# A fused causal convolution and multiplicative FFN on one core: order of the prologue's loads and first parts, and the place of the third convolution slot

## The chip, the core and the metric

One of the eight NeuronCores of a Trainium2 chip runs the whole program. Its engines run side by side and meet only at semaphores: the matrix engine (PE, with its weight loads shown apart as PEld), the vector engine (DVE), the scalar engine (ACT), GpSimd (POOL) and the sync engine (SP), which here only issues transfers. PE writes its results into PSUM; DVE and ACT carry them from there into SBUF, the working memory. The metric is the time of one execution on the device, in microseconds (us).

## The reference

```python
w = softmax(weight, over the 7 taps)                  # 8 heads x 7 taps
x_pad = zeros of 6 rows ahead of x                    # x: 8 x 3904 x 192
conv[b,s,h,:] = sum_k w[h,k] * x_pad[b,s+k,h,:]       # 24 channels a head
a = conv @ w1                                         # 192 -> 1024
b = conv @ w2                                         # 192 -> 1024
out = ((a * b) @ w3) @ w_out                          # 1024 -> 1024 -> 192
```

There are 31232 rows (tokens) of 192 channels. Inputs and output are float32; the kernel computes in bf16 with float32 sums. It multiplies w3 by w_out once (`W_sb`, 1024x192), so that a row needs two products: the first (`a` and `b`, and their elementwise product `abT`) and the second (`abT` by `W_sb`).

## The kernel before

**Tiles.** The rows are cut into two streams of 15616 (`NS = 2`), which lie on partitions 0 to 63 and 64 to 127. A *round* `R` is 512 rows of each stream; there are 31 rounds, in groups of four. The convolution works on *windows* of 64 rows, of which 58 are new, held in *blocks* of 6, 4, 8, 10, 8, six times 36, and 20 windows. It is a matmul too: per head a banded 64x64 matrix (`Aband`) times the window's 24 channels.

**The order is written by hand** (`tc.manual_schedule()`, line 65): each engine runs its instructions, and each queue its transfers, in the order of the program.

**PSUM** is one tile, `pairs`, of four pairs of banks. `banks()` (line 71) takes the first free pair off a list, `drained()` (line 78) appends it at the end when the code that empties it has been written.

**The prologue** (lines 136 to 560). The small `weight` is loaded (line 137), turned into a softmax by DVE and ACT (lines 216 to 224) and spread by a matmul; `diag`, a diagonal made by two selects on POOL (line 176), is multiplied by the taps (`band`, line 245) and summed by matmuls into `Aband`. The first quarter of w1 and w2 comes as float32 (`wfirst`, line 164) and is cast by ACT and POOL (`cast_w`); the other quarters come through POOL's queue (`load_w`), which also loads x (`load_x0`, line 171; `load_x`, line 105), all these with a cast. Block 0 is convolved (line 515) and transposed by PE into `xT` (line 517). Then, from line 521:

```python
    move_all(*conv(1, 0, H, "streams"), (A, V))
    first_tile(0)
    first_part(0, [0], 0, EARLY)
    move_all(*joint_transposes(1), (A, A, V))
    first_part(0, [1], 0, EARLY)
    first_part(0, [0, 1], EARLY, CH)
```

Block 1 is convolved and transposed here; `first_part` (line 403) is one part of a first product for columns of w1 and w2 in blocks of 128: two factors on PE (`first_factor`, twelve matmuls in all), a cast of the first by ACT (`first_cast`, line 386) and the product of the two by DVE (`first_times`, line 393). `EARLY` is 348, the rows of block 0. Blocks 2 to 4 are convolved among the first products of rounds 0 to 2. w3 is cast by a transfer into `w3rows`, and SP transposes it back in 16 pieces (`w3_transposes`, line 459). At line 557 POOL copies two values of `w3T`, which makes POOL wait for that piece before it issues the loads of blocks 5 and 6. `w3_product` (line 464) makes `W_sb`.

**The main loop** (line 579). A group has four first products (32 parts), then eight second products, one for each round and stream. Block `6 + p` is convolved in group `p`, head by head (`conv_heads`, line 566), in three *slots* of three, three and two heads, each placed behind one of the eight second products by `at` (line 590); DVE empties each head's pair. Behind the last slot the block is stored to `rows` in DRAM by SP (`store`); SP transposes it from there into `xT` during the next group (`send`, `transposes`), for the group after. Block 5 is convolved in the first group as well, behind its first three second products.

Of the kernel before, what the change touches and what calls it, by code (L numbers as in the profile page):

```python
# [16 lines left out]
def kernel(  # L17
# [10 lines left out]
    nc = tc.nc  # L28
# [49 lines left out]
    def drained(p):  # L78
        assert p not in free
        free.append(p)  # L80
# [53 lines left out]
                tiles.append((xb, 0))  # L134

    wall = const.tile([1, H, K], FP32)
    nc.scalar.dma_start(out=wall, in_=weight.rearrange("(o h) k -> o h k", o=1))

    n0 = SIZES[0] // 2
    xb0 = work.tile([128, 2 * n0, D], BF16, tag="xb", bufs=5, name="xb")  # L140
# [8 lines left out]
    diag = const.tile([128, Q + PAD], BF16)  # L149
    nc.vector.memset(zeros, 0.0)  # L150
    nc.vector.memset(tiny, 0.0)
    nc.vector.memset(ones, 1.0)  # L152
    nc.vector.memset(xb0[:, 0, :], 0.0)
    nc.vector.memset(half, 0.0)
    nc.vector.memset(half[:, Q:2 * Q], 1.0)
# [4 lines left out]
    wd = [const.tile([128, NP, DFF], BF16, name=f"wd{i}", tag=f"wd{i}") for i in range(2)]  # L160
    w_rows = [w.rearrange("(k q) f -> q k f", q=Q) for w in (moe_w1, moe_w2)]

    for i in range(2):
        nc.sync.dma_start(out=wfirst[:, i], in_=w_rows[i][:, :, 0:WC[1]])

    def load_w(part):
        cs = slice(WC[part], WC[part + 1])
# [3 lines left out]
    def load_x0(r):  # L171
        nc.gpsimd.dma_start(out=xb0[Q * r:Q * r + Q, 1:, :], in_=x_spans(r, 1, 2 * n0 - 1))  # L172

    load_x0(0)
    for p0 in (0, Q):
        nc.gpsimd.affine_select(  # L176
            out=diag[p0:p0 + Q], in_=ones[p0:p0 + Q].to_broadcast([Q, Q + PAD]),
            pattern=[[-1, Q + PAD]], compare_op=ALU.is_equal, fill=0.0, base=0,
            channel_multiplier=1)
    load_x0(1)  # L180
    for r in range(NS):
        nc.gpsimd.dma_start(out=xb0[Q * r + PAD:Q * r + Q, 0, :],  # L182
# [20 lines left out]
    def warm(n):  # L203
# [5 lines left out]

    warm(6)  # L210

    wmax = const.tile([1, H], FP32)
    wsum = const.tile([1, H], FP32)
    wrow = const.tile([1, H, K], BF16)
    wsb = const.tile([128, 2, 2, K], BF16)
    nc.vector.reduce_max(out=wmax, in_=wall, axis=AX.X)
    nc.vector.tensor_tensor(
        out=wall, in0=wall, in1=wmax.unsqueeze(2).to_broadcast([1, H, K]), op=ALU.subtract)
    nc.scalar.activation(out=wall, in_=wall, func=ACT.Exp)
    nc.vector.tensor_copy(out=ident[0:Q, 0:Q], in_=diag[0:Q, 0:Q])  # L220
    nc.vector.reduce_sum(out=wsum, in_=wall, axis=AX.X)
    nc.vector.reciprocal(out=wsum, in_=wsum)
# [268 lines left out]
    def move_all(p, moves, fs):  # L491
        for f, m in zip(fs, moves):
            move(f, m)
        drained(p)
# [22 lines left out]
    for k, f in enumerate((V, V, A)):  # L517
        p, *m = pe_transpose(0, k)
        move(f, m)
        drained(p)  # L520
    move_all(*conv(1, 0, H, "streams"), (A, V))
    first_tile(0)
    first_part(0, [0], 0, EARLY)
    move_all(*joint_transposes(1), (A, A, V))
    first_part(0, [1], 0, EARLY)
    first_part(0, [0, 1], EARLY, CH)
    load_w3(0)
    for i in range(2):
# [25 lines left out]
        3: seq([(pe_transposes, 4)])})  # L554
    store(4, need(GROUP - 1) - 1, queue=nc.gpsimd)
    nc.gpsimd.dma_start(out=wo_b, in_=wor)
    P(out=pace, in_=w3T[0:1, JT // 2 - 1, DFF - 2:DFF])
    load_x(5)
    load_x(6)
    first_product(3)  # L560
# [18 lines left out]
    for p, rounds in enumerate(groups):  # L579
        b = PROLOGUE_BLOCKS + p  # L580
        order = rounds[-1:] + rounds[:-1] if rounds[-1] == NR - 1 else rounds
        for j, R in enumerate(order if p else ()):
            first_product(R)
            send(R + GROUP)
            if j < 2 and b < NB:
                P(out=pace, in_=abT_of[R][0:1, JT - 1, 1, 0:2])  # L586
                load_x(b, (j,))
        if b < NB:
            zero(b)
        at = {1: [(b, slots[0])], 3: [(b, slots[1])], 5: [(b, slots[2])]}  # L590
        if p == 0:
            at = {0: [(5, slots[0], (V, A))], 1: [(5, slots[1], (V, A))],
                  2: [(5, slots[2], (V, A), need(GROUP))], 4: at[1], 5: at[3], 6: at[5]}
        for i, (R, r) in enumerate((R, r) for R in rounds for r in range(NS)):
            second_product(R, r, R == NR - 1 and r == 1, nc.sync if p else nc.gpsimd)
            for c in at.get(i, ()) if b < NB else ():
                conv_heads(*c)
            if p == 0 and i == 2:
                send(2 * GROUP - 1)
# [31 lines left out]
```

## Time and profile before

| | |
|---|---|
| runs shown | 521.29, 521.9, 522.05 us; median 521.9 |
| profiled execution | 522.07 us, of which the span from the first to the last instruction is 520.4 |
| granted PE clock | 1.00 |
| busy share of the span | PE 99%, PEld 65%, DVE 69%, ACT 63%, POOL 11% |
| DMA | 64.61 MB, mean 124 GB/s |

In the rows of the timeline stand the start in us, the time over which a merged row runs, the engine, the line and the operation, what is written and read, how many instructions the row merges, and in brackets the idle time ahead of it with what ended that. "POOLq", "SPq" and "ACTq" rows are instructions that a queue issues and that don't count as busy. In the chain of waits each piece has its start, its length and its name. Neighbouring matmuls overlap, so their distances are read from start to start.

### The profile page before, as it was taken

The numbers are of one execution on the slowest core, as the hardware profiler recorded it, in microseconds if no ns is written. First come the engines' busy times: TensorE is split into PE (matmuls) and PEld (weight loads), VectorE is DVE, ScalarE is ACT, GpSimd is POOL, SyncE is SP. The second block draws the span as 40 slices with busy tenths as digits, with TensorE's granted clock in tenths as the row PEclk, the third lists the DMA queues.
The fourth block names the chain that finished last, engine by engine and source line by source line (L and its number), as shares of the span: only waits on it lengthen the run. The fifth ranks groups of instructions, "written<-read, shape, count | busy, mean of one in ns | idle before, by whom it ended". The sixth has DMA issues, their size and how long they took to land.

```text
span 520.4 us, 13006 instructions
## 1 busy us (share of the span) xinstructions
PE 513.5 (99%) x5576; PEld 339.8 (65%) x5576; DVE 357.5 (69%) x343; ACT 325.7 (63%) x410; POOL 58.4 (11%) x98
## 2 busy tenths in 40 slices
PE   8999999999999999999999999999999999999997
PEld 4455788455885558845588455884558855599567
DVE  6778646899538994389943899438993299911970
ACT  6887643777437774377743777337774377734762
POOL 8501522130000200002000010001200000000000
PEclk9999999999999999999999999999999999999999
DMA  9979998699656973569645699456724532024004
GB/s 116 169 142 126 163 222 208 162 186 166 143 146 161 116 94 113 146 161 128 82 116 147 155 122 89 118 146 157 103 44 122 155 96 32 17 94 151 1 3 152
DMA packets 133420, 64.61 MB, mean 124 GB/s; under 512 B 90304, under 2 KB 132642, under 8 KB 133298
## 3 DMA queue, kind: packets, MB, share of 16 engines
q1 hardware_dynamic: 94320, 44.06, 36.1%
q0 software_dynamic: 38896, 19.62, 30.4%
q8 instruction: 43, 0.70, 0.6%
q14 instruction: 15, 0.12, 0.1%
q10 hardware_dynamic: 146, 0.10, 0.1%
HBM read 33.25 MB, written 36.52 MB: 134 GB/s over the span
## 4 chain that ended last, share of the span: by engine, by line
PE 95%; ACT 1%; DVE 1%; DMA 1%; POOL 1%; issue 0%; POOLq 0%; ACTq 0%
PE pairs L381 59%; PE pairs L432 32%; PE pairs L290 3%; DVE abT L400 1%; PE pairs L467 1%; ACT asb L389 1%; DMA xb<-in_x_dram 1%; PE pairs L343 0%; POOL xb L172 0%; POOL xb L182 0%; ACT convo L311 0%; POOL xb L119 0%; ACT xT L355 0%; POOL diag L176 0%; PE pairs L507 0%
## 5 line engine op out<-in xcount | busy, mean ns | idle before, releaser
L400 DVE TENSOR_TENSOR abT<-asb,pairs 128x1024 bf16<-128x1024 bf16 (+1 forms) x245 | 298.1, 1217 | 76.8 <-ACT asb L389 60.5
L381 PE MATMUL pairs<-xT,wd 64*128 64x512 bf16 (+3 forms) x3000 | 319.7, 371 | 0.7 <-DVE abT L400 0.3
L389 ACT CAST asb<-pairs 128x1024 bf16<-128x1024 f32 (+1 forms) x245 | 247.1, 1009 | 67.7 <-PE pairs L381 67.3
L381 PEld LDWEIGHTS <-wd 64*128 64x128 bf16 x3000 | 162.3, 94 | 151.8 <-issue 1.8
L432 PE MATMUL pairs<-W_sb,abT 128*128 128x192 bf16 x1952 | 166.1, 246 | 0.0
L432 PEld LDWEIGHTS <-abT 128*128 128x128 bf16 x1952 | 159.6, 98 | 9.7 <-issue 9.7
L437 ACT COPY osb<-pairs 128x384 f32<-128x384 f32 x122 | 58.3, 478 | 116.0 <-PE pairs L432 116.0
L311 DVE CAST convo<-pairs 128x864 bf16<-128x864 f32 (+5 forms) x67 | 50.8, 815 | 67.6 <-PE pairs L290 67.6
L119 POOL DMA_DIRECT2D xb<-in_x_dram x42 | 32.2, 781 | 7.6 <-PE pairs L381 4.1
L586 POOL COPY pace<-abT 1x2 bf16<-1x2 bf16 x10 | 1.7, 174 | 238.7 <-DVE abT L400 238.7
L290 PE MATMUL pairs<-xb,Aband 64*64 64x432 bf16 (+5 forms) x384 | 17.5, 284 | 0.4 <-DMA xb<-in_x_dram 0.3
L290 PEld LDWEIGHTS <-Aband 64*64 64x64 bf16 x384 | 7.2, 106 | 7.5 <-issue 6.3
L311 ACT CAST convo<-pairs 128x512 bf16<-128x512 f32 (+4 forms) x15 | 8.1, 584 | 0.5 <-PE pairs L290 0.4
L444 POOL DMA_DIRECT2D out_dram<-osb x8 | 6.1, 758 | 18.4 <-ACT osb L437 18.4
L437 DVE COPY osb<-pairs 128x192 f32<-128x192 f32 x1 | 0.4, 358 | 11.1 <-PE pairs L432 11.1
L467 PEld LDWEIGHTS <-w3T 128*128 128x128 bf16 x64 | 5.2, 98 | 0.4 <-issue 0.4
L467 PE MATMUL pairs<-wo_b,w3T 128*128 128x192 bf16 x64 | 5.5, 246 | 0.0
L190 POOL COPY wd<-wd 64x768 bf16<-64x768 bf16 x6 | 4.8, 847 | 0.0
L206 PE MATMUL pairs<-zeros 128*128 128x512 bf16 x8 | 3.7, 615 | 1.1 <-DVE ones L152 1.1
L343 PE MATMUL pairs<-ident,convo 128*128 128x128 bf16 x48 | 3.9, 219 | 0.7 <-DVE convo L476 0.5
L343 PEld LDWEIGHTS <-convo 128*128 128x128 bf16 x48 | 2.9, 97 | 2.5 <-issue 1.6
L469 ACT CAST W_sb<-pairs 128x192 bf16<-128x192 f32 x8 | 2.6, 320 | 2.8 <-PE pairs L467 2.8
(52 smaller groups left out, 38.6 us busy)
## 6 DMA issues: line engine op xcount, KB each, us to landing
out_dram<-osb SPq DMA_DIRECT2D x52, 384.0 KB
xb<-in_x_dram POOLq DMA_DIRECT2D x18, 432.0 KB, 7.8
rows<-convo SPq DMA_DIRECT2D x8, 648.0 KB
out_dram<-osb POOLq DMA_DIRECT2D x8, 384.0 KB, 4.9
w3rows<-in_moe_w_dram POOLq DMA_DIRECT2D x2, 1024.0 KB, 12.0
xb<-in_x_dram POOLq DMA_DIRECT2D x6, 240.0 KB, 5.4
rows<-convo SPq DMA_DIRECT2D x4, 324.0 KB
xT<-rows SPq DMA_TRANSPOSE x81
```

Source lines behind the costliest of these rows:

```text
L119: nc.gpsimd.dma_start(out=xb[Q * r:Q * r + Q, w:w + m, :], in_=x_spans(r, i, m))
L190: f(out=wd[i][Q:128, :, cs], in_=wd[i][0:Q, :, cs])
L290: nc.tensor.matmul(view(slice(Q * c, Q * c + Q), r)[:, :, j * G:(j + 1) * G], band_of(h, r), xb[Q * r:Q * r + Q, w0:w0 + n, h * G:(h + 1) ...
L311: f[e % len(f)](out=dst, in_=part)
L343: nc.tensor.transpose(out=tps[:, w, :], in_=convo[:, w, k].rearrange("p r g -> p (r g)"), identity=ident)
L381: nc.tensor.matmul(p[:, r, e * n:e * n + n], wd[i][rs, k, ft * 128:(ft + 1) * 128], xT[k][rs, r0 + c0:r0 + c1], start=(k == 0), stop=(k == ...
L389: nc.scalar.copy(out=asb, in_=pa)
L400: nc.vector.tensor_tensor(out=dst, in0=asb, in1=pb, op=ALU.mult)
L432: nc.tensor.matmul(ops[:, (g - g0) * D:(g - g0) * D + D], ab[:, jt, r, g * 128:(g + 1) * 128], W_sb[:, jt, :], start=(jt == 0), stop=(jt = ...
L437: f(out=osb[:, g0:g0 + per, :].rearrange("p g d -> p (g d)"), in_=ops[:, 0:per * D])
L444: queue.dma_start(out=out[t0:t0 + ng * 128, :].rearrange("(g p) d -> p g d", p=128), in_=osb)
L467: nc.tensor.matmul(wps[:, 0, 0:D], w3T[:, gt, jt * 128:(jt + 1) * 128], wo_b[:, gt, :], start=(gt == 0), stop=(gt == JT - 1))
```

## The change

- The small weight is loaded by SP instead of ACT, ahead of `wfirst`. Of `wfirst`, the half of w1 stays on SP and the half of w2 is issued by ACT, behind the Exp of the softmax. The softmax's first steps are written further up; on DVE and ACT they keep their place among the other work.
- `ones` is cleared to 1 by POOL instead of DVE, and POOL makes `diag` ahead of its first load of x instead of behind it.
- Block 1: its convolution stands behind the two factors of the first part instead of ahead of them, and its joint transposes behind the factors of the second part instead of ahead of them. DVE's products follow the convolution's and the transposes' evictions.
- POOL paces the loads of blocks 5 and 6 by piece 1 of the second half of w3's transposes instead of piece 3.
- In the main loop the third slot of blocks 6 to 11 stands behind the eighth second product of its group, that is, directly ahead of the next group's first products, instead of behind the sixth (in the first group: the seventh).

```diff
-    nc.scalar.dma_start(out=wall, in_=weight.rearrange("(o h) k -> o h k", o=1))
+    nc.sync.dma_start(out=wall, in_=weight.rearrange("(o h) k -> o h k", o=1))
...
-    nc.vector.memset(ones, 1.0)
...
-    for i in range(2):
-        nc.sync.dma_start(out=wfirst[:, i], in_=w_rows[i][:, :, 0:WC[1]])
+    nc.sync.dma_start(out=wfirst[:, 0], in_=w_rows[0][:, :, 0:WC[1]])
+    wmax = const.tile([1, H], FP32)
+    nc.vector.reduce_max(out=wmax, in_=wall, axis=AX.X)
+    nc.vector.tensor_tensor(
+        out=wall, in0=wall, in1=wmax.unsqueeze(2).to_broadcast([1, H, K]), op=ALU.subtract)
+    nc.scalar.activation(out=wall, in_=wall, func=ACT.Exp)
+    nc.scalar.dma_start(out=wfirst[:, 1], in_=w_rows[1][:, :, 0:WC[1]])
...
-    load_x0(0)
+    nc.gpsimd.memset(ones, 1.0)
     for p0 in (0, Q):
         nc.gpsimd.affine_select(
...
+    load_x0(0)
     load_x0(1)
...
-    wmax = const.tile([1, H], FP32)
...
-    nc.vector.reduce_max(out=wmax, in_=wall, axis=AX.X)
-    nc.vector.tensor_tensor(
-        out=wall, in0=wall, in1=wmax.unsqueeze(2).to_broadcast([1, H, K]), op=ALU.subtract)
-    nc.scalar.activation(out=wall, in_=wall, func=ACT.Exp)
...
+    first_tile(0)
+    a0 = first_factor(0, 0, [0], 0, EARLY)
+    c0 = first_cast(*a0)
+    b0 = first_factor(0, 1, [0], 0, EARLY)
     move_all(*conv(1, 0, H, "streams"), (A, V))
-    first_tile(0)
-    first_part(0, [0], 0, EARLY)
+    first_times(0, [0], 0, EARLY, c0, *b0)
+    a1 = first_factor(0, 0, [1], 0, EARLY)
+    c1 = first_cast(*a1)
+    b1 = first_factor(0, 1, [1], 0, EARLY)
     move_all(*joint_transposes(1), (A, A, V))
-    first_part(0, [1], 0, EARLY)
+    first_times(0, [1], 0, EARLY, c1, *b1)
     first_part(0, [0, 1], EARLY, CH)
...
-    P(out=pace, in_=w3T[0:1, JT // 2 - 1, DFF - 2:DFF])
+    P(out=pace, in_=w3T[0:1, 1, DFF - 2:DFF])
...
-        at = {1: [(b, slots[0])], 3: [(b, slots[1])], 5: [(b, slots[2])]}
+        at = {1: [(b, slots[0])], 3: [(b, slots[1])], 7: [(b, slots[2])]}
         if p == 0:
             at = {0: [(5, slots[0], (V, A))], 1: [(5, slots[1], (V, A))],
-                  2: [(5, slots[2], (V, A), need(GROUP))], 4: at[1], 5: at[3], 6: at[5]}
+                  2: [(5, slots[2], (V, A), need(GROUP))], 4: at[1], 5: at[3], 7: at[7]}
```

## The prediction

> **What bounds the kernel now.** I read the busy shares first, then the windows, then the timeline and the chain of waits of the stretches that the change touches.
>
> ```profile
> PE 513.5 (99%) x5576; PEld 339.8 (65%) x5576; DVE 357.5 (69%) x343; ACT 325.7 (63%) x410; POOL 58.4 (11%) x98
> ...
> 0.00:20.00 20.00, 17.46 (x337) 9.48 (x339) 14.03 (x34) 14.40 (x25) 18.69 (x33) 1.00 1.10 146
> 80.00:120.00 40.00, 40.00 (x409) 23.37 (x408) 34.17 (x32) 25.77 (x30) 7.88 (x12) 1.00 0.94 186
> ```
>
> The columns of a window are its length, the busy time (instructions) of PE, PEld, DVE, ACT and POOL, the granted clock, the DMA share and GB/s. PE is busy 99% of the span at full granted clock; in mid-run 40.00 of 40 us are full, and 2.5 us are missing in the first 20. So an edit pays only if it shortens PE's own stream or removes one of the few holes, and every delay of PE goes to the end. The change touches three places.
>
> **Place 1: the border between second and first products (six times).** PE's rows up to one border, DVE's row behind the slot, and three pieces of the chain of waits:
>
> ```profile
> 71.81 2.81 PE L432 MATMUL pairs<-W_sb,abT 128*128 128x192 bf16 x32
> 74.55 0.56 PE L290 MATMUL pairs<-xb,Aband 64*64 64x432 bf16 x8
> ...
> 143.49 0.74 PE L290 MATMUL pairs<-xb,Aband 64*64 64x432 bf16 x12
> 144.16 5.45 PE L432 MATMUL pairs<-W_sb,abT 128*128 128x192 bf16 x64
> 149.55 0.56 PE L290 MATMUL pairs<-xb,Aband 64*64 64x432 bf16 x8
> 150.04 5.46 PE L432 MATMUL pairs<-W_sb,abT 128*128 128x192 bf16 x64
> 155.42 41.62 PE L381 MATMUL pairs<-xT,wd 64*128 64x512 bf16 x384
> ```
>
> ```profile
> 149.97 2.02 DVE L311 CAST convo<-pairs 128x864 bf16<-128x864 f32 x2 [3.01 <-PE pairs L290]
> ```
>
> ```profile
> 16.26 1.23 DVE abT L400
> 17.49 0.04 issue
> 17.54 1.47 PE pairs L381 x12
> ...
> 90.57 41.55 PE pairs L381 x384
> ```
>
> From start to start, 64 second-product matmuls take 5.39 us (144.16 to 149.55) and 32 take 2.74 (71.81 to 74.55). So 32 more cost 2.65, and 5.39 - 5.30 = 0.09 us is left for going over to another tile shape. Twelve conv matmuls take 0.67 and eight 0.49, so four cost 0.18 and 0.13 is left. Today a block's third slot stands between two second products: 64x64 is entered and left, and later 128x128 is left for 64x128. At the border one of these three changes of shape falls away, 0.09 us. Blocks 6 to 11 have such a slot: 6 x 0.09 = 0.54 us.
>
> What takes it back is PSUM. The four pairs rotate in the order in which they were freed: behind the slot, the first two factors take the pairs of the last two second products, the third that of the slot's first head, the fourth that of its second head. DVE empties the two heads from 0.42 to 2.44 us after the slot's start (149.97 to 151.99, against 149.55). The first factors start at 0.49, a part of two factors takes 41.55/32 = 1.30, so the fourth factor wants its pair at 0.49 + 1.30 + 0.65 = 2.44, and PE follows a release by DVE by 0.05 (17.49 to 17.54). That is a stall of about 0.06. Net -0.03 at five borders, and -0.09 at the last, whose block is smaller (20 windows, not 36) and emptied in time: **-0.24 us**. Bounds: -0.54 without a stall, +0.1 with one twice as long. DVE's first product is ready at about the same 2.4 as DVE is free, so it is not late. In SP's queue the slot's stores now stand behind the last two output stores, and the next xT transposes wait for them; these are read one group later, 155.42 - 90.57 = 65 us on, which covers it. At the first border nothing moves on SP, which sends block 6's stores only 17 us behind it:
>
> ```profile
> 107.84 8.59 SPq L334 DMA_DIRECT2D rows<-convo  x4
> ```
>
> [...]
>
> **Place 2: block 5's slots among the first second products.**
>
> ```profile
> 67.37 1.09 PE L290 MATMUL pairs<-xb,Aband 64*64 64x432 bf16 x12
> ...
> L461 SPq DMA_TRANSPOSE w3T<-w3rows x16: 1190/1261/5104, 26.8 to 52.7; - x16
> ...
> 51.22 0.17 POOL L557 COPY pace<-w3T 1x2 bf16<-1x2 bf16 x1 [9.60 <-DMA w3T<-w3rows]
> ...
> 67.45 0.25 POOL L564 MEMSET xb<- 6x192 bf16 x1 [0.34 <-DMA xb<-in_x_dram]
> ```
>
> The first slot takes 1.09 us where one of the same twelve matmuls takes 0.74 (the row at 143.49): PE waits 0.35 us for block 5's load, whose last piece is cleared at 67.70. POOL holds that load until transpose 3 of the second half of w3 has landed, and the change until transpose 1. Two transposes of 1.26 us median are at most 2.5 us, at least 0; as SP issues them without a pause I take 1 us. Then the wait is gone; and if PE comes 0.35 or more late from place 3, the same wait absorbs it. Either way **-0.35**. The price: x traffic starts while more of w3's transposes are under way. The last is issued at 52.7, and the middle of the W_sb product, which reads its data, lies at 67.37 - 2.74 - 32 x 0.083 = 62.0, so 9 us cover it.
>
> **Place 3: the start.**
>
> ```profile
> 0.81 0.51 ACTq L137 DMA_DIRECT2D wall<-in_weight_dram  x1
> 0.82 1.40 SPq L164 DMA_DIRECT2D wfirst<-in_moe_w_dram  x2
> 1.32 0.85 POOL L172 DMA_DIRECT2D xb<-in_x_dram  x1 [0.80 <-POOLq L615]
> 2.26 0.59 POOL L176 TENSOR_SCALAR_AFFINE_SELECT diag<-ones 64x70 bf16<-64x70 bf16 x2
> 2.76 0.23 ACT L219 ACTIVATE wall<-wall 1x56 f32<-1x56 f32 x1
> 6.20 1.69 ACT L186 CAST wd<-wfirst 64x768 bf16<-64x768 f32 x2
> 8.14 0.85 PE L343 MATMUL pairs<-ident,convo 128*128 128x128 bf16 x9 [0.55 <-DVE convo L476]
> 9.03 0.45 ACT L476 COPY xT<-pairs 128x348 bf16<-128x348 bf16 x1 [0.55 <-PE pairs L343]
> 9.43 0.44 PE L290 MATMUL pairs<-xb,Aband 64*64 64x48 bf16 x31 [0.31 <-DMA xb<-in_x_dram]
> 9.80 1.06 PE L381 MATMUL pairs<-xT,wd 64*128 64x348 bf16 x12
> 10.79 0.51 PE L507 MATMUL pairs<-ident,convo 128*128 128x128 bf16 x6
> 11.22 0.61 ACT L476 COPY xT<-pairs 128x232 bf16<-128x232 bf16 x2
> 12.16 4.46 PEld L381 LDWEIGHTS <-wd 64*128 64x128 bf16 x60 [0.23 <-DVE abT L400]
> ```
>
> ```profile
> 2.00:3.00 1.00, 1.00 (x4) 0.35 (x3) 0.68 (x3) 0.98 (x3) 0.85 (x4) 1.00 0.41 119
> 3.00:4.00 1.00, 1.00 (x5) 0.23 (x4) 0.77 (x4) 0.00 (x0) 1.00 (x2) 1.00 1.19 196
> ```
>
> Today block 1's conv waits for its load until 9.43; then PE runs on without a hole: conv, first part, joint transposes (10.79), second part, and the next part from 12.16. The second part covers the copies that bring block 1 into xT (from 11.22, 0.43 after the transposes began, to 11.83).
>
> In the new order the first part stands ahead of that conv and covers its wait; but both parts stand ahead of the transposes, so nothing covers the copies. With arrivals as today: the third slice of xT is copied at 9.48, so the first part's last eight of twelve matmuls run from 9.53 and take 8/12 of 0.99 (9.80 to 10.79), to 10.19; conv takes 0.37 (9.43 to 9.80), to 10.56; the second part 0.99, to 11.55; then the transposes, and the copies from 11.98, the first done at 11.98 + 0.36 = 12.34, the second at 12.59. The next part begins at 12.38 instead of 12.16, and stops again for the second slice until 12.63, at matmuls that ran at about 12.25: **0.38 us late**. PE's later stalls up to 60 us are set by PE's own order (the piece at 16.26 above is one), so this is won back only at place 2.
>
> The arrivals move too. The first half of wfirst goes out behind the small weight on SP, some 0.5 later (the small one's issue took 0.51 on ACT); the second half waits on ACT behind the Exp (2.76), 1.3 later. POOL's first x load goes behind a memset and two selects, about 0.7; where these fit into POOL's idle time ahead of 1.32 it is 0.1 to 0.3 later, and the loads behind it go out between 0.4 earlier and 0.1 later. The DMA share is 1.19 from 3 us and 0.41 in the window from 2 to 3, so up to 0.4 us of DMA work is lost there, and block 0 arrives that much later. ACT's table load no longer stands behind a DMA issue, which brings the softmax about 0.1. I take +0.15, bounds -0.1 and +0.4. Place 3 in all: 0.38 + 0.15 = **+0.53** (0.28 to 0.8).
>
> [...]
>
> **Sum.** 0.53 - 0.35 - 0.24 = -0.06 us. The profiled execution took 522.07 us (span 520.4, and 1.7 around it), 0.17 over the median of the runs, 521.9. From there the forecast rounds to **521.9**, its own range 521.2 to 522.6.
>
> **Rivals.**
> 1. *The start gains.* If loads come no later and the copies are hidden after all, the hole from 8.99 to 9.43 is the gain, 0.44; with 0.35 and the full 0.54 it is 521.9 - 1.3 = 520.6. For it: that hole is real. Against: the third slice of xT is there at 9.48 and not before, in either order.
> 2. *The second half of wfirst is late on ACT's queue* (slower). ACT casts it ahead of its part of block 0's eviction: it is the second cast in the row at 6.20, at about 7.05. A landing after that holds ACT, then the transposes, then xT: each us late is a us of PE. At 8.3 it costs 1.2 more: 523.1. For it: it is issued 1.3 later into a full DMA. Against: today it is issued by 1.6 and read at 7.05, a long lead.
> 3. *The border stalls more than it saves* (slower). If it is the third factor that gets the pair of the second head, PE waits from 0.49 + 1.30 = 1.79 to 2.49 at five borders: 3.5 - 0.54 + 0.2 = 3.2, so 525.1. Against: the list of free pairs is first in, first out in the code.
> 4. *Pacing does not do what it says*: x comes no earlier, since the DMA is shared, or the last w3 transpose lands after 62.0. The first costs nothing as long as place 3 costs its 0.35; the second, for a transpose at 63, 1 us: 522.9.
>
> **Chances.** Forecast 0.52, start gains 0.20, late half 0.15, border 0.07, pacing 0.06. A measurement of this kernel can hardly tell a difference below about 0.2% (1.04 us) from no change. Faster by more is rival 1 alone, 0.20. Slower by more are rivals 2 and 3 and, from rival 4 and the forecast's upper tail, 0.05: 0.27. That leaves 0.53 within. The range reaches to rivals 1 and 2: 520.6 to 523.2.
>
> **What would show it.** Right: one part of block 0's columns ahead of block 1's conv; a hole of 0.2 to 0.4 us in PE's rows between the joint transposes and the next part, near 12.5; the first slot of block 5 in 0.74 us; at each border eight conv matmuls between L432 and L381, and DVE's first product no later behind them than PE's first part and cast allow. Wrong: the part behind the joint transposes under way before 12.0 (rival 1); ACT idle for wfirst after 7 us (rival 2); a group of first products of 42 us for 41.6 (rival 3); W_sb waiting for w3T at 62 us (rival 4).

## The result and the profile after

The changed kernel took 523.0 us (median of 22 runs, 522.55 to 525.55) where the kernel before took 522.15 beside it (22 runs, 521.11 to 523.21): a ratio of 1.0022, interval 1.0013 to 1.0031. So it is 0.2% slower. In the runs of this document a few executions, of the kernel before and of changed ones alike, took 894 to 1897 us; they are left out throughout. The profiled execution took 522.8, span 521.1, against 522.07 and 520.4 before.

The windows of the changed kernel (columns as before) show the same picture as before: PE full in mid-run, 2.6 us missing in the first 20, full clock.

```profile
0.00:20.00 20.00, 17.43 (x331) 9.37 (x333) 13.19 (x32) 13.75 (x23) 18.82 (x34) 1.00 1.06 146
80.00:120.00 40.00, 40.00 (x410) 25.34 (x409) 33.59 (x31) 25.78 (x30) 7.96 (x13) 1.00 0.94 185
```

The difference is in three short stretches and, in part of the executions, in the clock. First the start, PE's rows of the timeline and ACT's copies into xT (start, busy, engine, line, operation, tiles, shape, count, and the idle time before it with its releaser):

```profile
7.28 0.53 PE L290 MATMUL pairs<-xb,Aband 64*64 64x72 bf16 x32 [0.35 <-ACT wd L191]
8.42 0.85 PE L343 MATMUL pairs<-ident,convo 128*128 128x128 bf16 x9 [0.61 <-DVE convo L476]
9.20 1.37 PE L381 MATMUL pairs<-xT,wd 64*128 64x348 bf16 x12
10.50 0.44 PE L290 MATMUL pairs<-xb,Aband 64*64 64x48 bf16 x32
10.87 1.06 PE L381 MATMUL pairs<-xT,wd 64*128 64x348 bf16 x12
11.86 0.51 PE L507 MATMUL pairs<-ident,convo 128*128 128x128 bf16 x6
12.70 1.64 PE L381 MATMUL pairs<-xT,wd 64*128 64x164 bf16 x28 [0.33 <-DVE xT L476]
```

```profile
12.29 0.61 ACT L476 COPY xT<-pairs 128x232 bf16<-128x232 bf16 x2
```

Block 0's transposes start at 8.42, 0.28 later than before (8.14): its data arrived later. The row of the conv at 7.28 names ACT's cast of weights as what ended the wait, but the conv does not read what that cast writes, and before it started while that cast was still running. Block 0's last-but-one load of x, issued at 3.04, landed 4.1 later, at 7.14; before it was issued at 3.50 and landed 3.3 later, at 6.84. Block 0's conv in the kernel before:

```profile
6.97 0.62 PE L290 MATMUL pairs<-xb,Aband 64*64 64x72 bf16 x32
```

The first part now stands ahead of block 1's conv, as the change says, and the part behind the joint transposes waits for the copies: 12.70 where it was under way at 12.17. Matmul by matmul, PE is 0.67 us behind by 13.7 us: 0.31 from the arrivals (7.28 against 6.97) and 0.36 from the copies.

Then block 5's slot and one border, again PE's rows; and DVE's behind the border's slot:

```profile
68.36 0.74 PE L290 MATMUL pairs<-xb,Aband 64*64 64x432 bf16 x12
...
144.77 10.73 PE L432 MATMUL pairs<-W_sb,abT 128*128 128x192 bf16 x128
155.43 0.56 PE L290 MATMUL pairs<-xb,Aband 64*64 64x432 bf16 x8
...
155.93 41.75 PE L381 MATMUL pairs<-xT,wd 64*128 64x512 bf16 x384
```

```profile
155.93 2.02 DVE L311 CAST convo<-pairs 128x864 bf16<-128x864 f32 x2 [8.36 <-PE pairs L290]
157.89 2.46 DVE L400 TENSOR_TENSOR abT<-asb,pairs 128x1024 bf16<-128x1024 bf16 x2
```

Block 5's first slot takes 0.74 for 1.09: its wait is gone, 0.35 us. At the border the 128 second products take 10.66 from their start to the slot's, where 64 and 64 with a slot between took 5.39 and 5.38 and the slot 0.49: one change of shape is saved, about 0.1 us. But the 384 first products behind it take 41.75 for 41.62: 0.13 is given back at each of the four middle borders, 0.07 at the first and nothing at the last. From the end of the W_sb product to the last group of first products, the changed kernel takes 412.27 us (65.62 to 477.89) where before took 412.64 (64.64 to 477.27): 0.35 less from block 5's wait and 0.02 from all six borders.

One more piece comes near 35 us, where the change edits nothing (ACT's rows of the changed kernel, then of the kernel before):

```profile
33.67 1.01 ACT L389 CAST asb<-pairs 128x1024 bf16<-128x1024 f32 x1 [0.27 <-PE pairs L381]
35.30 1.01 ACT L389 CAST asb<-pairs 128x1024 bf16<-128x1024 f32 x1 [0.62 <-PE pairs L381]
```

```profile
33.01 1.01 ACT L389 CAST asb<-pairs 128x1024 bf16<-128x1024 f32 x1 [0.27 <-PE pairs L381]
34.31 1.01 ACT L389 CAST asb<-pairs 128x1024 bf16<-128x1024 f32 x1 [0.29 <-PE pairs L381]
```

The same cast starts 0.32 later than its data allows, and PE comes 0.99 behind instead of 0.67. The sum of the profiled execution: 0.67 + 0.32 - 0.35 - 0.02 = +0.62, which is what the last group of first products shows (477.89 against 477.27).

That explains 0.6 us but not the runs' spread: 14 of the 22 lie at 522.55 to 523.13 with a mean granted clock of 0.999 or 1.000, and 8 at 523.70 to 525.55 with 0.993 to 0.997.

### The profile page after: what moved, and what is told of

Its sections match the earlier page's. It is cut to its first block, busy times and chain, and to the rows that moved or that the text cites. A ratio compares the mean times of both kernels' runs of the same rounds, so it can differ in the third digit from the quotient of the medians.

```text
span 521.1 us, 13016 instructions
## 1 busy us (share of the span) xinstructions
PE 514.0 (99%) x5576; PEld 348.3 (67%) x5576; DVE 356.9 (69%) x342; ACT 325.5 (62%) x410; POOL 58.6 (11%) x99
## 4 chain that ended last, share of the span: by engine, by line
PE 96%; ACT 1%; DVE 1%; issue 0%; ACTq 0%; DVEq 0%
PE pairs L381 60%; PE pairs L432 31%; PE pairs L290 3%; PE pairs L467 1%; DVE abT L400 1%; ACT asb L389 1%; PE pairs L211 1%; PE pairs L343 1%; PE pairs L256 0%; ACT wd L191 0%; ACT convo L311 0%; DVE convo L476 0%; ACT xT L355 0%; PE pairs L507 0%; ACT osb L437 0%
## 5 line engine op out<-in xcount | busy, mean ns | idle before, releaser
L381 PEld LDWEIGHTS <-wd 64*128 64x128 bf16 x3000 | 170.5, 94 | 146.2 <-issue 5.5
```

The source lines that it names most:

```text
L381: nc.tensor.matmul(p[:, r, e * n:e * n + n], wd[i][rs, k, ft * 128:(ft + 1) * 128], xT[k][rs, r0 + c0:r0 + c1], start=(k == 0), stop=(k == ...
```

## The experiments

Up to four kernels ran together on one chip and shared the runs of the kernel before. "At half clock" counts the executions whose mean granted clock is 0.997 or less; by the records one stretch of 3.41 us at 0.5 in 521 us is 0.5 x 3.41/521 = 0.003 of the mean, two are 0.007. In the profile of the kernel before the clock is at 0.50 behind the last matmul as well (the window from 520.03 us to the end), and e2's profile, with one stretch in its first 20 us, has a mean of 0.995; so up to 0.002 of a mean is put down to the end, an estimate from these numbers.

| run | median us | ratio to before, interval | at half clock |
|---|---|---|---|
| e1 before again | 521.94 | 1.0007, 0.9995 to 1.0019 | 0 of 12 |
| e2 changed kernel again | 524.37 | 1.0048, 1.0029 to 1.0067 | 6 of 6 |
| e3 order alone | 522.46 | 1.0007, 0.9998 to 1.0017 | 0 of 12 |
| e4 changed, order as before | 523.36 | 1.0030, 1.0016 to 1.0043 | 8 of 12 |
| e5 loads alone | 522.97 | 1.0019, 1.0006 to 1.0033 | 6 of 11 |
| e6 POOL's part of the loads | 522.84 | 1.0009, 0.9997 to 1.0020 | 6 of 11 |
| e7 the weights' part of the loads | 525.2 | 1.0062, 1.0049 to 1.0076 | 6 of 6 |
| e8 changed, five warming matmuls | 522.88 | 1.0017, 1.0007 to 1.0026 | 0 of 11 |
| e9 pacing alone | 522.11 | 1.0008, 0.9997 to 1.0019 | 2 of 12 |
| e10 border alone | 522.08 | 1.0001, 0.9992 to 1.0011 | 0 of 11 |
| e11 border, second head on ACT | 521.53 | 0.9998, 0.9985 to 1.0012 | 1 of 11 |
| e12 best of the parts | 521.7 | 0.9999, 0.9989 to 1.0009 | 0 of 11 |
| e13 e7 with seven warming matmuls | 523.01 | 1.0009, 0.9993 to 1.0025 | 0 of 11 |
| e14 changed, loads as before | 522.54 | 0.9996, 0.9981 to 1.0012 | 0 of 12 |
| e15 e12 again | 522.53 | 0.9997, 0.9978 to 1.0015 | 1 of 11 |

The runs of the kernel before that stood beside these had 2 of 29, 1 of 27, 1 of 35 and, on the chip of e13 to e15, 8 of 29 at half clock.

### e1 to e4: which half of the change, and the spread of the runs

e1 and e2 are the two kernels unchanged. e3 is the kernel before with only block 1's new order; e4 is the changed kernel without it:

```diff
# e3: the kernel before with
+    first_tile(0)
+    a0 = first_factor(0, 0, [0], 0, EARLY)
+    c0 = first_cast(*a0)
+    b0 = first_factor(0, 1, [0], 0, EARLY)
     move_all(*conv(1, 0, H, "streams"), (A, V))
-    first_tile(0)
-    first_part(0, [0], 0, EARLY)
+    first_times(0, [0], 0, EARLY, c0, *b0)
...
# e4: the changed kernel with these lines as before
```

> The kernel before, unchanged, to see the granted clock of each of its runs. The changed kernel's 22 runs fall into two groups: 14 at 522.55 to 523.13 us with a mean granted clock of 0.999 to 1.000, and 8 at 523.70 to 525.55 with 0.993 to 0.997. If the second group belongs to the change (holes in PE's work near 7 to 8 us that delay the full clock), these runs all stand at 0.999 to 1.000 and within about 521.1 to 523.2. If it belongs to the chip of the day, about a third of these runs show 0.993 to 0.997 as well and are 1 to 2.5 us longer than the others.

> The changed kernel, unchanged, for a second profile. The stall of 0.33 us ahead of the part at 37.6 us, where ACT starts a cast 0.3 us late, belongs to the program if it is there again at the same place, and to that one execution if it is not. Elsewhere PE's rows agree with the first profile to 0.1 us from 14 us on: 0.67 us late to 36 us, 0.35 regained at block 5's first slot, 0.04 lost at each of the four middle borders. Granted clock below 0.998 in about a third of the runs, and ratio 1.001 to 1.003.

> The kernel before with only the new order of block 1 (its convolution and its joint transposes behind the factors); loads, pacing and border as before. If uncovered copies are the loss, convolution of block 0 starts at 6.97 as before, the part behind the joint transposes starts at 12.4 to 12.5 instead of 12.17 and goes on without a hole from 12.6 to 12.7: 0.35 to 0.4 us late, all of it absorbed at block 5's first slot, so about 522.1. The rival, that the new order gains the wait for block 1's load (0.44 us), has that part start by 11.8.

> The changed kernel with only the order of block 1 as before. Loads are as in the changed kernel, where block 1 landed at 7.9 us instead of 9.4. If the order alone costs the start its copies, block 1's convolution now starts without a wait at about 9.2 and the part behind it at 11.9 to 12.0, that is 0.2 us ahead of the kernel before and 0.7 to 0.9 ahead of the changed kernel; with block 5's wait gone it ends 0.3 to 0.5 us ahead of the kernel before. If the loads are the loss, it is as late as the changed kernel, 0.3 us behind the kernel before at 12.2.

Measured: the order costs at most a little (e3, 1.0007), and none of its 12 executions has a half clock; e4, which has the loads and not the order, is 1.0030 with 8 of 12 at half clock, and e2 has 6 of 6 where a third was expected. e3's start, PE's rows:

```profile
7.01 0.59 PE L290 MATMUL pairs<-xb,Aband 64*64 64x72 bf16 x32
...
12.47 1.86 PE L381 MATMUL pairs<-xT,wd 64*128 64x164 bf16 x30 [0.33 <-DVE xT L476]
```

With block 0's conv at 7.01 as before, the part behind the transposes waits to 12.47 for 12.17: this is the uncovered copy, without any arrival. ACT's cast near 35 us is late by the same 0.3 in e2, e3 and e14, all with the new order, and in time in e1 and e4, without it. But e8 below, which has the order and five more matmuls, is in time as well (its casts start at 34.27 and 35.58). So that stall was seen only with the new order, and not always with it; no row of these traces names what the cast waits for, and the cause stays open.

e2's windows, cut where its clock changes:

```profile
5.44:8.86 3.42, 1.83 (x124) 1.40 (x117) 2.26 (x6) 3.23 (x7) 2.80 (x5) 1.00 1.22 161
8.86:12.27 3.41, 3.41 (x53) 2.08 (x53) 0.84 (x3) 1.31 (x3) 3.41 (x6) 0.50 0.99 118
12.27:15.68 3.41, 3.07 (x60) 2.11 (x54) 2.41 (x4) 2.52 (x5) 3.41 (x6) 1.00 1.07 128
```

The granted clock is 0.50 for 3.41 us and then 1.00 in the windows read behind it, up to 20 us. Block 0's conv comes later than in the profile above, and it waits for x:

```profile
7.67 0.53 PE L290 MATMUL pairs<-xb,Aband 64*64 64x72 bf16 x32 [0.74 <-DMA xb<-in_x_dram]
```

In e4 the clock is 0.50 for twice as long, 8.12 to 14.94. This is what the profiled execution of the changed kernel happened not to show. In e2's stretch ahead of it PE is busy for only 1.83 of 3.42 us. Two theories were left: the clock falls because PE idles too much early (A), or because of the DMA's load or the late data as such (C).

e1 shows where the kernel before gets its own spread; its profiled execution took 523.16 at full clock:

```profile
58.89 3.39 PE L467 MATMUL pairs<-wo_b,w3T 128*128 128x192 bf16 x39
63.51 2.24 PE L467 MATMUL pairs<-wo_b,w3T 128*128 128x192 bf16 x25 [1.23 <-DMA w3T<-w3rows]
```

PE waits 1.2 us for w3's transposes in the middle of the W_sb product. The forecast counted 9 us of cover there. In e3 and in the changed kernel PE reaches this product 1.2 us or more later (60.09 and 60.33) and does not wait; their undisturbed runs lie within 0.6 us of one another, all but one in e3.

### e5 to e8: which load, and the clock

```diff
# e5: the kernel before with all edits to the loads
# e6: only these
-    nc.vector.memset(ones, 1.0)
...
-    load_x0(0)
+    nc.gpsimd.memset(ones, 1.0)
     for p0 in (0, Q):
...
+    load_x0(0)
# e7: only the small weight on SP, the softmax moved up, the second half of wfirst on ACT
# e8: the changed kernel with
+    warm(2)
     move_all(*conv(0, 0, 4, ()), (V, V))
     move_all(*conv(0, 4, 4, ()), (A, A))
+    warm(3)
```

> The kernel before with all the edits to the loads and nothing else (small weight on SP, second half of wfirst on ACT behind the Exp, memset of ones and selects on POOL ahead of block 0's load); the order of block 1, the pacing and the border are as before. Theory A (the loads alone bring the half clock): block 0's conv starts 0.3 to 0.7 later than 7.0, and in at least a third of the executions the mean granted clock is below 0.9985, with a stretch of 3.41 us at 0.5 between 8 and 15 us; median 0.8 to 2 us above the kernel before. Theory B (the loads are harmless, the half clock needs another part of the change): no execution below 0.9985, the time within 0.5 us of before.

> The kernel before with only POOL's part of the loads: the memset of ones goes to POOL and the two selects stand ahead of block 0's first load. Theory A1 (block 0's x comes later because of POOL's order): block 0's conv starts at 7.3 to 7.7 and waits for xb, and the clock falls in some executions. Theory A2 (it comes later because the weights' requests stand ahead of it in the DMA engines): conv at 7.0 as before, clock at 0.999 or above in all executions, time within 0.4 us of before.

> The kernel before with only the weights' part of the loads: small weight on SP, first half of wfirst behind it, softmax moved up, second half of wfirst on ACT behind the Exp. Theory A2: block 0's conv starts at 7.3 to 7.7 and the clock falls in some executions. Theory A1: conv at 7.0 to 7.1 and no execution below 0.9985.

> The changed kernel with five more warming matmuls of 512 columns on zeros: two ahead of block 0's conv and three ahead of its transposes, in the two stretches of 0.55 and 0.81 us in which PE is idle. They compute nothing that is used. Theory A (PE's early rows leave too much idle time, so the granted clock falls for the next 3.41 us): the clock stays at 0.999 or above in all executions and the median is 1 to 2 us under that of the changed kernel on this chip (524.4), at 522.4 to 523.2. Rival C (the clock falls for another reason, for example the load of the DMA): as many executions below 0.9985 as in the changed kernel, and the time as there or longer.

Measured: the loads alone do it (e5), and each part does some of it; e6's time is not clear of no change, but 6 of its 11 executions are at half clock. Block 0's conv in e6, e7 and e5 in turn, and its wait:

```profile
7.36 0.54 PE L290 MATMUL pairs<-xb,Aband 64*64 64x72 bf16 x32 [0.44 <-DMA xb<-in_x_dram]
```

```profile
8.12 0.77 PE L290 MATMUL pairs<-xb,Aband 64*64 64x72 bf16 x32 [1.19 <-DMA xb<-in_x_dram]
```

```profile
7.87 0.62 PE L290 MATMUL pairs<-xb,Aband 64*64 64x72 bf16 x32 [0.94 <-DMA xb<-in_x_dram]
```

It waits for its own x, not for the weights whose requests were moved. The DMA columns of the window from 2 to 3 us say a part of how (share and GB/s at the end of the row), for the changed kernel, e7 and e6, with e7's requests of the timeline:

```profile
2.00:3.00 1.00, 1.00 (x4) 0.34 (x3) 0.68 (x4) 0.55 (x3) 1.00 (x2) 1.00 0.11 18
```

```profile
2.00:3.00 1.00, 1.00 (x4) 0.35 (x3) 0.73 (x4) 0.55 (x3) 0.85 (x4) 1.00 0.08 24
```

```profile
2.00:3.00 1.00, 1.00 (x4) 0.35 (x3) 0.49 (x3) 0.99 (x3) 1.00 (x2) 1.00 0.38 103
```

```profile
1.22 0.73 SPq L163 DMA_DIRECT2D wfirst<-in_moe_w_dram  x1
2.65 0.71 ACTq L169 DMA_DIRECT2D wfirst<-in_moe_w_dram  x1
```

In the changed kernel and e7 the DMA share is 0.11 and 0.08 for 0.41 before: wfirst's first request goes out at 1.22 instead of 0.82, behind the small weight, and e7's second half at 2.65 on ACT. By the difference of the shares 0.3 us of DMA work is lost there. That is not all of it: e6 loses next to nothing from 2 to 3 us (0.38), and its conv still waits 0.44, although POOL issues its last loads of block 0 at 3.04 for 3.50. Later windows of the same traces show other gaps: e6's share from 4 to 5 us is 0.98 for 1.24 before, 0.3 us of work, and e7's from 4 to 5 and from 5 to 6 us are 1.09 and 0.63 for 1.24 and 1.22, another 0.7 us, which with the first 0.3 makes up about e7's 1.1 us at the conv. Why the DMA engines do less there, with x's requests out and not yet landed, no row says; so how the requests' order delays x is shown only in part.

e7's and e8's windows:

```profile
4.68:8.09 3.41, 1.85 (x113) 1.31 (x113) 2.35 (x6) 2.50 (x5) 2.84 (x5) 1.00 1.11 143
8.09:11.50 3.41, 2.88 (x77) 2.24 (x79) 1.74 (x5) 1.87 (x5) 3.41 (x6) 0.50 1.14 140
11.50:14.92 3.42, 3.42 (x28) 1.72 (x24) 1.38 (x3) 1.65 (x5) 3.42 (x6) 0.50 1.30 144
```

```profile
4.23:7.65 3.42, 2.40 (x115) 1.43 (x114) 2.80 (x6) 2.15 (x5) 2.56 (x5) 1.00 1.36 187
7.65:11.06 3.41, 3.22 (x56) 1.72 (x56) 1.50 (x4) 2.11 (x5) 3.41 (x6) 1.00 0.86 103
```

In e8 the DMA is as full as in e2 and e7 or fuller (1.36 in the first window for 1.22 and 1.11) and x as late as in e2 or later (conv at 7.82 for 7.67), but five matmuls on zeros shorten the holes (two run ahead of the wait for x, of which 0.57 is left), and none of 11 executions is at half clock; 522.88 is 1.5 us below e2, on the same chip. The requests are those of the changed kernel, so what is left, 1.0017, is about the change's cost at full clock. Block 0's conv in e8:

```profile
7.82 0.58 PE L290 MATMUL pairs<-xb,Aband 64*64 64x72 bf16 x32 [0.57 <-DMA xb<-in_x_dram]
```

(Two of e8's executions have 0.998, its profiled one among them, whose windows from 4.2 to 20 us are all at 1.00; 0.002 is less than the 0.003 of one stretch.)

### e9 to e12: pacing, border, and the parts that pay

```diff
# e9
-    P(out=pace, in_=w3T[0:1, JT // 2 - 1, DFF - 2:DFF])
+    P(out=pace, in_=w3T[0:1, 1, DFF - 2:DFF])
# e10, at both places; e11 has 7: [(b, slots[2], (V, A))]
-        at = {1: [(b, slots[0])], 3: [(b, slots[1])], 5: [(b, slots[2])]}
+        at = {1: [(b, slots[0])], 3: [(b, slots[1])], 7: [(b, slots[2])]}
# e12: e9, e11 and
     move_all(*conv(0, 4, 4, ()), (A, A))
+    warm(3)
```

> The kernel before with only the pacing of block 5's load changed (POOL waits for transpose 1 of the second half of w3, not 3). Theory (the forecast's place 2): block 5's first slot spans 0.40 us from first to last matmul start, where before it spans 0.75 to 0.89, so 0.35 to 0.5 us less; no wait for w3T inside the W_sb product (one execution of the kernel before had 1.47 us there), because nothing of it is made later: median 521.2 to 521.6 against 521.8 to 522.1. Rival: x and the last transposes share the DMA engines, so what block 5 wins is lost as a wait of 1 us or more for w3T near 62 us in most executions: median 522.5 or more.

> The kernel before with only the third slot of each block moved to the border. Theory (as the trace of the changed kernel has it): the group of 384 first products behind the slot spans 41.31 us at the first border, 41.38 at the next four and 41.24 at the last, against 41.24 before, and each border saves 0.095 of shape change: in all between -0.1 and +0.1 us, so the time is within 0.3 us of before. The forecast's working: groups of 41.30, in all -0.24. Rival (the stall comes from other parts of the change): groups of 41.24 at all six, in all -0.57.

> As the one before, but of the slot's two heads the second is emptied by ACT while DVE empties the first. Theory (the stall is the wait of the fourth factor for the pair of the second head, which DVE empties last): the pair is free 0.8 us earlier, the groups span 41.24 at all borders and -0.5 to -0.57 us in all remain: median 521.2 to 521.5 against 521.8 to 522.1. Rival (DVE's first product or ACT's first cast sets it): ACT now comes 0.2 to 0.5 later to the first cast, and the groups span 41.4 or more.

> The kernel before with its own loads and its own order of block 1, with the new pacing, the border with the second head on ACT, and three more warming matmuls of 512 columns on zeros (they compute nothing that is used) ahead of block 0's transposes, where PE is idle for 0.75 us. If the parts are what the experiments say: -0.35 to -0.5 from the pacing, -0.5 from the border, 0 from the warming matmuls in time, with no execution below 0.9985 in the granted clock: median 520.7 to 521.3, and no execution above 522.5. If the parts take each other's gain: 521.4 or more.

Measured in the medians: nothing that these runs can tell from no change, in any of the four. In the traces there is more. Block 5's first slot in e9, and the clearing that releases it:

```profile
67.24 0.96 PE L290 MATMUL pairs<-xb,Aband 64*64 64x432 bf16 x12
```

```profile
50.08 0.18 POOL L557 COPY pace<-w3T 1x2 bf16<-1x2 bf16 x1 [8.59 <-DMA w3T<-w3rows]
...
67.20 0.25 POOL L564 MEMSET xb<- 6x192 bf16 x1 [0.29 <-DMA xb<-in_x_dram]
```

POOL's pace comes 1.14 earlier than before (51.22), but x is cleared only 0.25 earlier (67.20 for 67.45): from the pace to the clearing it takes 17.12 us, 16.23 before. So the wait shrinks by 0.13 (0.96 for 1.09), not by 0.35. Both numbers of the expectation were missed: neither a gain in the median nor the rival's wait in the profiled execution.

e10 has the border groups of the changed kernel from the second on (41.75 there; the first takes 41.82 for 41.69), nearly as the theory said, and its median moved by nothing. Its profile and e11's hold a wait for w3T as in e1: the W_sb product spans 6.45 and 5.97 us from first to last matmul start, for 5.21 in the kernel before. In e11 ACT empties the second head; ACT's and DVE's rows there:

```profile
156.09 0.88 ACT L311 CAST convo<-pairs 128x864 bf16<-128x864 f32 x1
156.86 1.02 ACT L389 CAST asb<-pairs 128x1024 bf16<-128x1024 f32 x1
```

```profile
155.92 1.06 DVE L311 CAST convo<-pairs 128x864 bf16<-128x864 f32 x1 [8.35 <-PE pairs L290]
157.97 3.67 DVE L400 TENSOR_TENSOR abT<-asb,pairs 128x1024 bf16<-128x1024 bf16 x3 [0.99 <-ACT asb L389]
```

The pair is free 0.98 sooner (156.97 for 157.95), and the groups are 41.62 at the first border and 41.70 at the second. So most of the first border's stall was that pair; at the middle borders the pair's earlier release wins 0.05 of 0.13. The expectation of no stall at all was missed: from first to last matmul start the first two groups take 41.25 and 41.33, for 41.24 without a stall. What holds the other 0.08 was not tried; DVE's first product starts 0.08 later than in the changed kernel (157.97 for 157.89), behind ACT's later cast. Block 5's share taken off, e11 keeps 0.33 us of the some 0.6 that six changes of shape are worth.

e12 ends 1.1 us earlier in its trace (span 519.4 against 520.4; 476.19 for 477.27 at the last group of first products): 0.33 from the borders, 0.35 from block 5, and 0.41 because block 1's load came early in that execution, so that the conv there did not wait. But 4 of its 11 runs took 522.25 to 522.87, where none above 522.5 was expected, and the median is 521.7, not 521.3 or less.

### e13 to e15: the two open questions

```diff
# e13: e7 with
+    warm(4)
     move_all(*conv(0, 0, 4, ()), (V, V))
     move_all(*conv(0, 4, 4, ()), (A, A))
+    warm(3)
# e14: the changed kernel with its loads as before; e15: e12 again
```

> The kernel with only the weights' part of the loads (e7, where block 0's conv came at 8.12 and the clock was at 0.5 for 6.83 us, median 525.2), with seven more warming matmuls of 512 columns on zeros: four ahead of block 0's conv, three ahead of its transposes. They compute nothing that is used. Theory A (idle PE lets the clock fall): block 0's conv still waits for its x until about 8.1, but no execution shows 3.41 us or more at 0.5 (mean clock 0.998 or above in all), and the median falls by 1.5 to 2.5 us to 522.8 to 523.7; what is left over the kernel before is the late arrival alone, about 1 us. Rival C (the clock falls because of the DMA's load or of the late arrival itself): clock 0.993 and a median of about 525 as in e7.

> The changed kernel without its edits to the loads: the new order of block 1, the border and the pacing are in. Theory (the loads bring the late arrival and the half clock, the rest of the change about cancels): block 0's conv at 7.0 to 7.1, no execution below 0.998, median 522.2 to 522.6, as the order alone had (522.46), that is 0.3 to 0.6 above before. Rival (order, border and pacing cost by themselves what the changed kernel lost): 523 or more.

> The kernel of e12 once more, for its interval (0.9999, 0.9989 to 1.0009; its profiled execution ended 1.1 us before that of the kernel before). If pacing and border gain 0.6 to 1.0 us in the executions without a late w3T: ratio 0.998 to 0.9995. If the spread of the executions (521.1 to 523.4) hides it or takes it back: 0.9995 to 1.0005.

Measured: e13 has 0 of 11 at half clock where e7 had 6 of 6, and its median is 2.2 us lower, though on another chip, on which the kernel before itself was at half clock in 8 of 29 runs and reached 525.7. The requests are e7's. Whether its conv still came at 8.1 was not seen. e14 has no half clock either, and 522.54 stands beside 522.53 of a kernel before whose median holds those disturbances; its own conv is at 6.92, and 9 of its 12 runs lie within 522.40 to 522.79. e3, with the order alone, has nearly the same median (522.46), so border and pacing add little to it; beside its own kernel before (521.78) e3 is 0.7 higher in the median and 0.4 by the ratio, whose interval reaches 0.9998. So the order's cost at full clock is between nothing and 0.7. e15 again shows no gain in the median (0.9997), with its runs in two groups, 521.06 to 521.24 and 522.53 to 523.21, and one at half clock.

### e16 to e18: e12's kernel three times more

> The kernel of e12 and e15 once more, one look, to meet one of the executions of 522.2 to 523.2 beside those of 521.1 at a full clock. Theory (w3T late): in such an execution PE waits 0.7 to 1.5 us for w3T inside the W_sb product, as in e1 (523.16) and e10 (522.92), so that this product spans 5.9 to 6.7 us from first to last matmul start, not 5.21. Rival: the product spans 5.21 and the time goes elsewhere (the start, block 5's load, or behind the last matmul). In an execution of 521.1 both expect 5.21.

> The kernel of e12 again, a second look. Theory (w3T late): an execution above 522.2 shows a W_sb product of 5.9 to 6.7 us from first to last matmul start. Rival: 5.21 there, and the time elsewhere. At 521.1 both expect 5.21.

> The kernel of e12 again, a third look. Theory (w3T late): an execution above 522.2 shows a W_sb product of 5.9 to 6.7 us from first to last matmul start. Rival: 5.21 there, and the time elsewhere. At 521.1 both expect 5.21.

Measured: 521.31, 521.73 and 521.15 beside 522.13 of the kernel before. These are one execution each. None took 522.2 or more, so what the longer executions wait for stays open: w3T as in e1, e10 and e11 is likely but was not seen in this kernel. Most of the difference between the three is block 5's first slot. In the second of them PE's rows are

```profile
67.04 0.37 PE L290 MATMUL pairs<-xb,Aband 64*64 64x432 bf16 x3
67.63 0.70 PE L290 MATMUL pairs<-xb,Aband 64*64 64x432 bf16 x9 [0.22 <-POOL xb L565]
```

and the slot spans 0.95 us there from first to last matmul start, 0.71 and 0.46 in the other two, 0.40 in e12. With the new pacing the wait is anything from 0 to 0.55.

## Why the prediction was wrong

The step that failed is the start: the lateness of block 0's x was put at +0.15 us and nothing behind it, where x came 0.31 to 0.66 late and 8 of 22 and 6 of 6 executions were at half clock. The prediction forecast 521.9, no change, as 0.53 - 0.35 - 0.24 = -0.06; the trace has +0.99 - 0.35 - 0.02 = +0.62, and beyond that comes the clock. Of the 0.68 between the two sums, 0.32 is the stall at ACT's cast, 0.22 the border and 0.14 the start. 523.0 lies inside the range, but by terms other than those that the range was made for; the likeliest case, no change, was the wrong one.

- **Place 3, the copies: right.** Forecast 0.38, measured 0.36 in the changed kernel; e3 shows the same wait by itself. "The next part begins at 12.38 instead of 12.16": it began at 12.70, with everything 0.31 later.
- **Place 3, the arrivals: the term that failed first.** "I take +0.15, bounds -0.1 and +0.4". Measured +0.31 in the profiled execution and +0.66 on the chip of e2 (7.67, against 7.01 in e3 on the same chip). The forecast looked at the DMA window from 2 to 3 us and took a middle value, although most of the work in that window was lost (0.11 for 0.41); and it looked no further, where e6 and e7 have gaps between 4 and 6 us. The weights' part alone delays x by 1.1 us (e7). This and the +0.66 lie outside the bounds.
- **What late arrivals trigger: not foreseen at all.** The forecast asked for the granted clock, found 1.00 in each window and went on. It did not ask what holes in PE's early rows do to the clock. PE waits for late x (0.44 to 1.19 us in e2 and e4 to e7), and in these five profiles it then runs at a clock of 0.50 for 3.41 to 6.83 us. e8 and e13, which put matmuls into the holes and leave the requests as they are, have 0 of 11 executions at half clock each, where e2 and e7 have 6 of 6; e5 to e7 have it without the rest of the change. So in these runs the half clock goes with PE's holes, and not with the moved requests by themselves.
- **"PE's later stalls up to 60 us are set by PE's own order ... so this is won back only at place 2": half right.** Nothing was won back before, but another 0.32 was lost at ACT's cast near 35 us, in four of the five traces that have the new order of block 1 (not in e8). The forecast put this at nothing; its cause stays open.
- **Place 2: the number right, the reason only in part.** The wait is gone (0.74), but e3 has no wait either with the old pacing, since PE comes later; and pacing alone takes 0.13 (e9). "If PE comes 0.35 or more late from place 3, the same wait absorbs it" is what happened.
- **Place 1: the saving right, the stall too small.** The 0.09 per change of shape stands, or a little more. The stall was put at 0.06; it is 0.07 at the first border and 0.13 at the four middle ones, none at the last, as forecast. The difference is in DVE's row above: it starts 0.50 behind the slot's start (155.93 against 155.43), not 0.42, and so ends at 2.52, not 2.44. By the forecast's own working that makes 0.13; but e11, which frees the pair 0.98 sooner, keeps 0.08 of it, so the pair is not the only limit there. Six borders gain 0.02, not 0.24, which is inside the bounds.
- **Rivals.** Rival 1's hole ahead of block 1's conv is not there in every execution (none in e1, e10 and e12), so its gain is not always to be had. Rival 2 gave nearly the right time, 523.1, by a mechanism that did not happen: ACT's cast waits for nothing at 7 us, and x is late instead. (In e5, e7 and e8 it does wait 0.2 to 0.6 for that half, but x comes later still, so it costs nothing there.) Rival 3 is of the right kind and far too large. Rival 4's late w3T is real in an execution of the kernel before (e1) and in two of kernels with its start (e10, e11); in the traces of the change, with its later PE, it is not there.

## What to carry to other kernels

Requests at the very start were worth more here than their issue time: moves of 0.2 to 1.0 us, some later and some earlier, brought block 0's x from 0.3 to 1.1 us later, by a way that these runs show only in part. Before an edit to a start that is bound by arrivals, read how long PE is idle there, not only which clock one profile shows: here PE was busy for 1.83 to 2.31 of the 3.41 us ahead of each half clock that a profile shows, and with five matmuls on zeros in the holes 0 of 11 executions were at half clock (e8), where 6 of 6 were without them (e2). A profile is one execution: list the clock of every run before a difference of 0.2% is explained from one trace.

## What the runs showed of the hardware

At the start of this kernel the granted clock is 0.50 for 3.41 us in the profiles of e2 and e6 and for 6.82 to 6.83 us in those of e4, e5 and e7; it falls at 8.86 (e2), 8.12 (e4), 8.48 (e5), 8.47 (e6) and 8.09 us (e7). In the 3.41 us ahead of that PE was busy for 1.83 (e2), 1.85 (e7), 2.10 (e6), 2.15 (e5) and 2.31 us (e4). In 14 other profiles (all but e13's), each read in three windows of 3.41 us that cover the holes around 7 and 8 us, PE was busy for 2.37 us or more in each window, and the clock is 1.00 in all of them. The two rows nearest to each other, e4's and that of the changed kernel's profiled execution:

```profile
4.70:8.12 3.42, 2.31 (x145) 1.74 (x144) 2.33 (x6) 2.75 (x5) 2.73 (x6) 1.00 1.33 183
```

```profile
6.16:9.57 3.41, 2.37 (x101) 1.59 (x95) 2.38 (x7) 2.71 (x6) 3.19 (x5) 1.00 1.08 126
```

The kernel before had 2.50 and 2.66 us in two profiles, at 1.00, and a few of its runs are at half clock too (2 of 29, 1 of 27, 1 of 35 and 8 of 29 above). Of the first 3.41 us at half clock, those with PE busy for 2.80 to 2.88 us (e4, e5, e7) were followed by as much again at 0.50, those with 3.37 and 3.41 (e6, e2) by 1.00.

This is what was measured at this start; no limit of busy time can be read from it. In e1 a window of the same length holds the wait for w3T and is emptier than e4's, and yet the mean granted clock of that execution is 1.000:

```profile
61.15:64.57 3.42, 2.19 (x27) 1.97 (x25) 0.00 (x0) 0.99 (x4) 0.00 (x0) 1.00 1.29 130
```

It holds 27 matmuls, mostly of 128x128 by 192 columns, where the two windows above hold 145 and 101, mostly of 64x64. So busy time as the profile counts it is not all that differs between a window ahead of 0.50 and one ahead of 1.00; what else counts, no run tests.

The longest wait in PE's rows ahead of a half clock was 1.19 us (e7's conv row above), so no long hole stood ahead of it. That matmuls on zeros in the holes took the half clock away is the result of e8 and e13, 0 of 11 executions each.
